# A decode step of two transformer layers: the last product of layer 1 is laid out by result columns, takes the residual in, and is written as four rows

## The chip, the cores and the metric

The program runs on one core of a Trainium2 chip. Its engines are TensorE (PE in the profile, with its weight loads listed as PEld), VectorE (DVE), ScalarE (ACT), GpSimd (POOL) and SyncE (SP); 16 DMA engines carry the core's transfers. The metric is the device time of one execution in microseconds, given as the median of several runs. Less is better.

## The reference

One token (a row x of 640 values, bfloat16) goes through two layers of attention and two of a gated feed-forward block. Both layers use the same weights and the same caches:

```
x = x + A(layernorm(x))      # layer 0
x = x + B(layernorm(x))
x = x + A(layernorm(x))      # layer 1
x = x + B(layernorm(x))
A: q = x @ wq (32 heads of 192); scores against the last 4096 keys of each head,
   softmax, weighted sum of the values, then @ wo
B: out = (silu(x @ w1) * (x @ w3)) @ w2       # w1, w3: 640 x 1536; w2: 1536 x 640
```

The change concerns the last line of the last layer: the product with w2, the sum with x, and the write of the 640 results.

## The kernel before

**Data.** All large operands stream from HBM through an arena of 16 slots in SBUF, each 128 partitions by 6144 bfloat16 values (1536 KB). A list `loads` fixes the order of the transfers; `refill` (L184 to L195) issues the next ones on SP's queue whenever a slot has come free, and `done` (L209) gives a slot back. For each layer the list holds the pages of wq, the K and V pages of 32 heads, six pages of wo, and four pages of the feed-forward weights: `fa` and `fb` (w1 and w3, first four fifths), `fc` (the rest of w1 and w3, and w2's chunks 0 to 3), and `fd` (w2's chunks 4 to 10). Chunk 11 of w2 stays in a buffer of its own, `keep`, from layer 0 on. A chunk is 128 rows of w2, 640 columns wide, 160 KB.

`fd` is loaded in two transfers, of 3840 columns (chunks 4 to 9, 960 KB) and of 640 columns (chunk 10, 160 KB). They are the last two loads of the program.

**The residual.** x is kept as `xsq[:, 0:5]` in float32: value 5p + c of x stands in partition p, column c.

**Products of one row.** With only one token, each product has a stationary operand of one column. TensorE's array is therefore used as four groups of 32 columns: `tile_position=(0, 32 * j)` places a product in group j, and its one row of results lands on PSUM partition 32j. In the w2 product (L421 to L431), chunk `fcx` goes to group `fcx % 4`; the 640 result columns are two halves of 320, each in a PSUM tile of its own. So every group holds a partial sum over three of the twelve chunks, for all 640 columns. `y_open` first fills the two tiles with a product of a zero operand, eight instructions of 320 columns, so that the other partitions are zero.

**From partial sums to the residual.** `y_to_residual` (L228 to L236) copies the two PSUM tiles to SBUF as bfloat16 (one on ScalarE, L230, one on VectorE, L231), multiplies the copy's columns with a column of ones in five small products (tile `yt_ps`), which adds the four partial rows and brings value 5p + c to partition p, column c, and adds `xsq` on VectorE (L235). In layer 1 this last sum goes to `ob`, bfloat16, 128 by 5, and one transfer on SP's queue (L474) writes it to HBM: 128 pieces of 10 bytes.

**Order.** `pin` keeps the instructions of each engine in the order of the program text, and each engine runs its own in that order, waiting on semaphores. All products are issued by the helper `mm`, so they all carry line L75; they are told apart by their tiles: `g_ps`, `u_ps` (products with w1 and w3), `gt_ps` (their transposes), `htd` (the gated values, bfloat16, 12 columns of 128, written by L418), `y_ps`, `yt_ps`, `st_ps` (the layer norm's sums, a float32 product), `rl_ps` (sums of the softmax, a float32 product). SP's queue issues loads alone until the output transfer. POOL writes constants at the start (L93 to L127) and later copies parts of `wst`; it has nothing to do in the last feed-forward block.

Of the kernel before, what the change touches and what calls it, by code (L numbers as in the profile page):

```python
# [7 lines left out]
BF16 = mybir.dt.bfloat16  # L8
F32 = mybir.dt.float32
U32 = mybir.dt.uint32  # L10
ALU = mybir.AluOpType
# [4 lines left out]
P = 128  # L16
D = 640
NCH = 5
# [6 lines left out]
PGW = 6144  # L25
# [17 lines left out]
def kernel(  # L43
# [13 lines left out]
    nc = tc.nc  # L57
# [3 lines left out]
    cst = ctx.enter_context(tc.tile_pool(name="cst", bufs=1))  # L61
# [3 lines left out]
    ps_a = ctx.enter_context(tc.tile_pool(name="ps_a", bufs=2, space=PSUM))  # L65
# [4 lines left out]
    def pin(ins):  # L70
        tc.keep_in_program_order(ins)
        return ins

    def mm(*a, **k):
        return pin(nc.tensor.matmul(*a, **k))  # L75
# [9 lines left out]
    xsq = cst.tile([P, 12], F32, name="xsq")  # L85
# [9 lines left out]
                            pattern=[[-32, 4]], channel_multiplier=1)  # L95
# [3 lines left out]
                            pattern=[[-32, 4], [-1, 4]], channel_multiplier=1)  # L99
# [4 lines left out]
    for j in range(4):  # L104
        nc.gpsimd.affine_select(out=sel[:], in_=sel[:], compare_op=ALU.not_equal, fill=1.0, base=-(32 * j + 14),
                                pattern=[[-1, 2], [2, HB], [0, 16]], channel_multiplier=1)
    lsel = cst.tile([64, HB, 16], F32, name="lsel")
    nc.gpsimd.memset(lsel[:], 0.0)
    for blk in range(8):
        nc.gpsimd.affine_select(out=lsel[:], in_=lsel[:], compare_op=ALU.not_equal, fill=1.0, base=-(8 * blk + 7),  # L110
                                pattern=[[1, HB], [0, 16]], channel_multiplier=1)
    mask = cst.tile([P, 16], BF16, name="mask")
    nc.gpsimd.memset(mask[:], 0.0)
    for hl in range(HB):
        nc.gpsimd.affine_select(out=mask[:], in_=mask[:], compare_op=ALU.not_equal, fill=1.0, base=-16 * hl,
                                pattern=[[-1, 16]], channel_multiplier=1)
# [6 lines left out]
    ptm = cst.tile([P, 16 * 144], BF16, name="ptm")  # L123
    otd = cst.tile([P, 48], BF16, name="otd")
    htd = cst.tile([P, 12], BF16, name="htd")
    zero = cst.tile([P, 32], BF16, name="zero")
    nc.gpsimd.memset(zero[:], 0.0)  # L127
    w20 = cst.tile([P, 768], BF16, name="w20")
    qt_sb = cst.tile([P, 2, 6, 16], BF16, name="qt_sb")


    cst.tile([P, 80], BF16, name="pad")
    arena = arn.tile([P, NSLOT * PGW], BF16, name="arena")
    keep = arn.tile([P, 640], BF16, name="keep")
    rest = arn.tile([P, PGW - NSTASH], BF16, name="rest")
    free = list(range(NSLOT))
    home = {}
    loads = []
# [5 lines left out]
    w2_v = B_w2.rearrange("(p f) n -> p (f n)", f=12)  # L144
# [12 lines left out]
    for layer in range(2):  # L157
        for c in range(NCH):
            loads.append((("q", layer, c), [(0, PGW, wq_v[c])]))
        for i in range(H + LEAD):  # L160
            for kind, g, cache in (("v", i - LEAD, A_v_cache), ("k", i, A_k_cache)):
                if not 0 <= g < H:
                    continue
                h = (k_head if kind == "k" else head)(layer, g)
                if kind == "k" and layer == 1 and h in RETAIN:
                    if h == STASH:
                        loads.append((("k", 1, h), []))
                    continue
                loads.append(((kind, layer, h),
                              [(0, PGW, cache[0, h, S0:SK, :].rearrange("(p t) d -> p (t d)", p=P))]))  # L170
        for w in range(6):
            parts, ci, end = [], 9 * w, min(9 * w + 9, 48)
            while ci < end:
                to = min(end, ci - ci % 12 + 12)
                parts.append((640 * (ci - 9 * w), 640 * (to - ci),
                              wo_v[ORDER[layer][ci // 12]][:, 640 * (ci % 12):640 * (ci % 12 + to - ci)]))
                ci = to
            loads.append((("o", layer, w), parts))
        loads.append((("fa", layer), [(0, PGW, w1_v[:, 0:PGW])]))
        loads.append((("fb", layer), [(0, PGW, w3_v[:, 0:PGW])]))  # L180
        loads.append((("fc", layer), [(0, 1536, w1_v[:, PGW:]), (1536, 1536, w3_v[:, PGW:]),
                                      (3072, 2560, w2_v[:, 0:2560])]))
        loads.append((("fd", layer), [(0, 3840, w2_v[:, 2560:6400]), (3840, 640, w2_v[:, 6400:7040])]
                      + [(None, 640, w2_v[:, 7040:7680])] * (layer == 0)))  # L184

    def refill():
# [18 lines left out]
    def page(key):  # L205
        return arena[:, home[key] * PGW:home[key] * PGW + PGW]

    def done(key):
        free.append(home.pop(key))  # L209
        refill()  # L210
# [14 lines left out]
        pin(nc.vector.tensor_scalar(out=xs[:, :, 3], in0=xsq[:, 0:NCH],  # L225
                                    scalar1=st[:, 0:1], scalar2=rstd[:], op0=ALU.subtract, op1=ALU.mult))

    def y_to_residual(y_ps, dst=None):  # L228
        y_sb = w20
        pin(nc.scalar.copy(out=y_sb[:, 0:320], in_=y_ps[0][:, 0:320]))  # L230
        pin(nc.vector.tensor_copy(out=y_sb[:, 320:640], in_=y_ps[1][:, 0:320]))  # L231
        yt_ps = ps_m.tile([P, NCH], F32, tag="m", name="yt_ps")
        for c in range(NCH):
            mm(yt_ps[:, c:c + 1], lhsT=y_sb[:, c:D:NCH], rhs=onesb[:], start=True, stop=True)
        pin(nc.vector.tensor_tensor(out=(xsq[:, 0:NCH] if dst is None else dst), in0=xsq[:, 0:NCH], in1=yt_ps[:],  # L235
                                    op=ALU.add))  # L236

    def qproj(layer):
        q_ps = ps_a.tile([P, 512], F32, tag="a", name="q_ps")
# [125 lines left out]
    def y_open(name):  # L365

        y_ps = [ps_a.tile([P, 512], F32, tag="a", name=f"{name}{i}") for i in range(2)]
        for nh in range(2):
            for j in range(4):
                mm(y_ps[nh][32 * j:32 * j + 32, 0:320], lhsT=zero[:], rhs=ptm[:, 0:320],  # L370
                   start=True, stop=False, tile_position=(0, 32 * j))
        return y_ps
# [12 lines left out]
            done(("o", layer, w))  # L385
        y_to_residual(y_ps)

    def ffn(layer, dst=None):
        g_ps = ps_a.tile([P, 512], F32, tag="a", name="g_ps")
        u_ps = ps_a.tile([P, 512], F32, tag="a", name="u_ps")  # L390
        for ps, kind, c0, c1, off in ((g_ps, "fa", 0, 4, 0), (u_ps, "fb", 0, 4, 0),
                                      (g_ps, "fc", 4, 5, 0), (u_ps, "fc", 4, 5, 1536)):
            pg = page((kind, layer))
            for c in range(c0, c1):
                for j in range(4):
                    mm(ps[32 * j:32 * j + 32, 0:384], lhsT=xs[:, c, 3:35],
                       rhs=_ap(pg, 0, P, off + 1536 * (c - c0) + 3 * j, [[12, 128], [1, 3]]),
                       start=(c == 0), stop=(c == NCH - 1), tile_position=(0, 32 * j))
            if kind != "fc":
                done((kind, layer))  # L400
        gu = w20.rearrange("p (g n) -> p g n", g=2)
        pin(nc.scalar.copy(out=gu[:, 0, :], in_=g_ps[:, 0:384]))
        pin(nc.vector.tensor_copy(out=gu[:, 1, :], in_=u_ps[:, 0:384]))
        gt_ps = ps_m.tile([P, 2, 3, 4], F32, tag="m", name="gt_ps")
        for gi in range(2):
            for k in range(3):
                mm(gt_ps[:, gi, k, :], lhsT=gu[:, gi, k:384:3], rhs=sel4[:], start=True, stop=True)
        ex = sml.tile([P, 12], F32, tag="ex", name="ex")
        pin(nc.scalar.activation(out=ex[:], in_=gt_ps[:, 0, :, :].rearrange("p k j -> p (k j)"), func=ACTF.Exp,
                                 scale=-1.0))  # L410
        ut = sml.tile([P, 12], F32, tag="ut", name="ut")
        pin(nc.vector.tensor_copy(out=ut[:], in_=gt_ps[:, 1, :, :].rearrange("p k j -> p (k j)")))
        gut = sml.tile([P, 12], F32, tag="gut", name="gut")
        pin(nc.vector.tensor_tensor(out=gut[:], in0=gt_ps[:, 0, :, :].rearrange("p k j -> p (k j)"), in1=ut[:],
                                    op=ALU.mult))
        pin(nc.vector.tensor_scalar_add(out=ex[:], in0=ex[:], scalar1=1.0))
        pin(nc.vector.reciprocal(out=ex[:], in_=ex[:]))
        pin(nc.vector.tensor_tensor(out=_ap(htd[:], 0, P, 0, [[1, 3], [3, 4]]),  # L418
                                    in0=gut[:].rearrange("p (k j) -> p k j", k=3),
                                    in1=ex[:].rearrange("p (k j) -> p k j", k=3), op=ALU.mult))  # L420
        y_ps = y_open("y2_ps")  # L421
        for fcx in range(12):
            j = fcx % 4
            pg, off = (page(("fc", layer)), 3072 + 640 * fcx) if fcx < 4 else (page(("fd", layer)), 640 * (fcx - 4))
            if fcx == 11:
                pg, off = keep, 0
            for nh in range(2):
                mm(y_ps[nh][32 * j:32 * j + 1, 0:320], lhsT=htd[:, fcx:fcx + 1], rhs=pg[:, off + 320 * nh:off + 320 * nh + 320],
                   start=False, stop=(fcx >= 8), tile_position=(0, 32 * j))
            if fcx == 3:  # L430
                done(("fc", layer))  # L431
        done(("fd", layer))
        y_to_residual(y_ps, dst)

    def attention(layer):
        layernorm()
# [29 lines left out]
        wo_proj(layer)  # L466

    refill()
    ob = cst.tile([P, NCH], BF16, name="ob")
    for layer in range(2):  # L470
        attention(layer)
        layernorm()
        ffn(layer, dst=(ob[:] if layer == 1 else None))
    nc.sync.dma_start(out=out[0, 0, :].rearrange("(p c) -> p c", c=NCH), in_=ob[:])  # L474


# [28 lines left out]
```

## Time and profile before

The kernel takes 537.86 us (median of three runs, 534.64 to 539.17). The profiled execution took 536.54 us; its span, from the first instruction to the last, is 534.4 us, so 2.1 us lie outside the span.

| | of the profiled execution |
|---|---|
| span | 534.4 us |
| DMA, mean over the span | 417 GB/s, 222.77 MB |
| PE busy | 288.6 us (54%) |
| DVE busy | 225.7 us (42%) |
| ACT busy | 41.8 us (8%) |
| POOL busy | 14.6 us (3%) |
| mean granted TensorE clock | 0.685 of full speed |

The DMA engines are busy for 90% or more in every fortieth of the span but the first (80%) and the last (30%). In the last 13 us the profile shows, from 521 us on, the gated products, the w2 product, the residual sum, and the output transfer, which is issued at 530.82 us. In the profile's rows, "x 8" is a count of instructions, "[0.71 <-DMA ...]" the idle time of the engine before the group and what ended it; the time of one matmul overlaps that of the next ones.

### The profile page before, as it was taken

Reading aid. Unit: us, or ns where it says so; the run is one execution under the profiler, and the core shown is the slowest. Engines: PE = TensorE matmul, PEld = TensorE weight load, DVE = VectorE, ACT = ScalarE, POOL = GpSimd, SP = SyncE. Lnnn points to the kernel's source line nnn. Section 1 sums busy time; section 2 is a strip of 40 time slices with the busy share of each in tenths; the row PEclk is TensorE's granted clock in tenths of the full one; section 3 lists DMA queues with packets and bytes.
Section 4 is the critical chain, followed back from the end, with each engine's and each line's share of the span. In section 5 each row is a group of like instructions: output and inputs, shape, how many; then the busy total and the mean of one; then the engine's idle time right before and its main releaser. Section 6 shows DMA issues by size and latency. Waiting matters only on the chain.

```text
span 534.4 us, 5680 instructions
## 1 busy us (share of the span) xinstructions
PE 288.6 (54%) x2400; PEld 118.7 (22%) x2400; DVE 225.7 (42%) x271; ACT 41.8 (8%) x107; POOL 14.6 (3%) x52
## 2 busy tenths in 40 slices
PE   2365364556554656553545366595556756734544
PEld 1121121222221222211212122252222222211121
DVE  1189765465455764520011058507444654410011
ACT  1100200011001100020000010203001100020000
POOL 5000000000000000000000000000000000000000
PEclk9989798657766575665556558887885776565556
DMA  8999999999999999999999999999999999999993
GB/s 347 429 430 429 432 426 430 428 431 431 426 432 426 433 427 430 430 418 432 421 415 418 428 373 407 425 428 431 432 426 429 428 433 428 428 429 430 428 421 153
DMA packets 22633, 222.77 MB, mean 417 GB/s; under 512 B 2768, under 2 KB 3152, under 8 KB 5456
## 3 DMA queue, kind: packets, MB, share of 16 engines
q1 hardware_dynamic: 22464, 222.41, 98.4%
q8 instruction: 19, 0.31, 0.2%
q14 instruction: 6, 0.05, 0.0%
q10 hardware_dynamic: 144, 0.00, 0.0%
HBM read 222.40 MB, written 0.00 MB: 416 GB/s over the span
## 4 chain that ended last, share of the span: by engine, by line
DMA 80%; PE 11%; DVE 6%; ACT 1%; issue 1%; POOL 0%; SPq 0%; DVEq 0%; ACTq 0%; POOLq 0%
DMA arena<-in_A_k_cache_dram 50%; DMA arena<-in_A_v_cache_dram 13%; DMA arena<-in_A_wo_dram 8%; DMA arena<-in_B_w_dram 5%; DVE arena L286 4%; PE s_ps L75 4%; DMA arena<-in_A_wq_dram 4%; PE pss L75 2%; PE o_ps L75 2%; DMA xb<-in_A_x_dram 1%; PE y_ps L75 1%; PE q_ps L75 1%; ACT w L316 0%; DVE t L301 0%; PE u_ps L75 0%
## 5 line engine op out<-in xcount | busy, mean ns | idle before, releaser
L286 DVE STREAM_TRANSPOSE arena<-arena 128x1536 uint32<-128x1536 uint32 x100 | 171.3, 1754 | 96.6 <-DMA arena<-in_A_k_cache_dram 96.4
L75 PE MATMUL pss<-arena,wst 128*32 128x512 bf16 x480 | 108.3, 539 | 107.4 <-DVE arena L286 104.7
L75 PE MATMUL o_ps<-arena,ptm 128*16 128x384 bf16 (+1 forms) x1024 | 124.8, 458 | 29.3 <-DMA arena<-in_A_v_cache_dram 27.6
L75 PEld LDWEIGHTS <-wst 128*32 128x32 bf16 x768 | 55.1, 116 | 234.7 <-issue 195.9
L75 PE MATMUL s_ps<-arena,wst 128*32 128x512 bf16 x288 | 54.7, 502 | 34.0 <-DVE arena L286 28.5
L75 PEld LDWEIGHTS <-ptm 128*16 128x16 bf16 (+2 forms) x1036 | 47.1, 107 | 72.9 <-issue 64.0
L359 DVE SCALAR_TENSOR_TENSOR w<-ot_ps,rl,mask 128x192 bf16<-128x192 f32 x8 | 3.3, 418 | 57.4 <-PE ot_ps L75 57.4
L75 PE MATMUL y_ps<-arena,otd 128*1 128x320 bf16 x192 | 17.2, 458 | 16.3 <-DMA arena<-in_A_wo_dram 16.3
L311 ACT ACTIVATE tb<-m 32x32 f32<-32x32 f32 x8 | 1.8, 228 | 297.7 <-DVE m L308 297.7
L75 PE MATMUL q_ps<-arena,xs 128*32 128x384 bf16 x160 | 14.5, 519 | 18.8 <-DMA arena<-in_A_wq_dram 16.1
L329 ACT COPY ptm<-w 32x128 bf16<-32x128 bf16 x40 | 16.1, 403 | 26.3 <-PE o_ps L75 24.1
L231 DVE CAST w<-y_ps 128x320 bf16<-128x320 f32 x4 | 2.0, 491 | 38.2 <-PE y_ps L75 38.2
L75 PEld LDWEIGHTS <-xs 128*32 128x32 bf16 x240 | 9.3, 125 | 36.9 <-issue 27.9
L256 DVE CAST ptm<-q_ps 128x768 bf16<-128x768 f32 x2 | 1.9, 958 | 31.7 <-ACT w L254 31.7
L275 POOL COPY wst<-qt_sb 32x48 bf16<-32x48 bf16 x16 | 6.2, 385 | 232.8 <-PE pss L75 188.0
L75 PEld LDWEIGHTS <-otd 128*1 128x1 bf16 x192 | 6.6, 102 | 26.8 <-issue 22.6
L301 DVE TENSOR_REDUCE t<-s_ps 64x1 f32<-64x512 f32 x3 | 2.0, 682 | 17.8 <-PE s_ps L75 17.8
L301 DVE TENSOR_REDUCE t<-pss 64x1 f32<-64x512 f32 x5 | 3.4, 681 | 12.9 <-PE pss L75 12.9
L319 DVE STREAM_TRANSPOSE w<-w 64x512 bf16<-64x512 bf16 x8 | 5.6, 705 | 7.2 <-ACT w L316 7.2
L75 PE MATMUL ot_ps<-w,sel 128*128 128x192 bf16 x16 | 3.4, 309 | 8.7 <-ACT w L353 7.9
L353 ACT CAST w<-o_ps 128x384 bf16<-128x384 f32 x8 | 3.8, 478 | 54.5 <-PE o_ps L75 51.7
L75 PE MATMUL st_ps<-xsq,onesD 128*128 128x12 f32 x8 | 2.3, 367 | 9.4 <-DVE xsq L213 9.4
(78 smaller groups left out, 101.2 us busy)
## 6 DMA issues: line engine op xcount, KB each, us to landing
arena<-in_A_v_cache_dram SPq DMA_DIRECT2D x64, 1536.0 KB, 29.2
arena<-in_A_k_cache_dram SPq DMA_DIRECT2D x50, 1536.0 KB, 29.2
arena<-in_A_wq_dram SPq DMA_DIRECT2D x10, 1536.0 KB, 10.5
arena<-in_A_wo_dram SPq DMA_DIRECT2D x6, 1440.0 KB, 15.9
arena<-in_B_w_dram SPq DMA_DIRECT2D x4, 1536.0 KB, 13.9
arena<-in_A_wo_dram SPq DMA_DIRECT2D x4, 960.0 KB, 16.6
arena<-in_A_wo_dram SPq DMA_DIRECT2D x6, 480.0 KB, 14.4
arena<-in_B_w_dram SPq DMA_DIRECT2D x2, 960.0 KB, 13.1
```

The lines of the kernel that those rows point to most:

```text
L75: return pin(nc.tensor.matmul(*a, **k))
L231: pin(nc.vector.tensor_copy(out=y_sb[:, 320:640], in_=y_ps[1][:, 0:320]))
L256: pin(nc.vector.tensor_copy(out=q_rep[par][:], in_=src))
L275: pin(nc.gpsimd.tensor_copy(out=dst, in_=src))
L286: pin(nc.vector.transpose(x[:, w * sp:w * (sp + 1)].bitcast(U32), x[:, w * sp:w * (sp + 1)].bitcast(U32)))
L301: pin(nc.vector.reduce_max(out=t0[:, 0:1], in_=s_ps[0:64, :], axis=AX.X))
L311: pin(nc.scalar.mul(out=tb[32:64, :].rearrange("p (a z) -> p a z", a=4), in_=mb, mul=-SCALE))
L319: pin(nc.vector.transpose(et[:], e[:]))
L329: pin((eng.copy if eng is nc.scalar else eng.tensor_copy)(out=dst, in_=src))
L353: pin(nc.scalar.copy(out=o_sb[:, 0:384], in_=o_ps[:, 0:384]))
L359: pin(nc.vector.scalar_tensor_tensor(out=om, in0=ot_ps[:], scalar=rl[:], in1=mask[:].unsqueeze(2).broadcast_to([P, 16, 12]), op0=ALU.mult, ...
```

## The change

Layer 0 is left as it is. In layer 1:

- The third load of `fd` appears: its 3840 columns come as 2560 (chunks 4 to 7) and 1280 (chunks 8 and 9), and then the 640 columns of chunk 10.
- A function `last_rows` takes the place of the w2 product, the two copies, the five `yt_ps` products, the sum on VectorE and the output transfer. Group j now takes result columns 160j to 160j + 159 of every chunk: twelve chunks by four groups, 48 products of 160 columns, all into one PSUM tile `f_ps`. Four products with a zero operand open it.
- x is added inside that tile: for each of the five columns c of `xsq` and each group j, a float32 product of `xsq[:, c]` with 32 columns of an identity matrix writes the values 5p + c of the group to every fifth column. These are 20 float32 products, each of 32 columns. They stand on PE after the `gt_ps` products and the zero products, and before the first product with `htd`.
- The identity, 128 by 128 float32, is made by two instructions on POOL, in the arena slot that has been free for longest; all loads have been issued by then.
- The chunks are taken in the order 0, 1, 2, 3, 11, 4, ..., 10.
- One copy on VectorE brings 128 partitions by 160 columns to SBUF as bfloat16, and one transfer on SP's queue writes partitions 0, 32, 64 and 96 to HBM: four rows of 320 bytes.
- The buffer `ob` is gone, and the unused buffer `pad` grows from 80 to 96 columns; the arena begins at the same address as before.

```
-        loads.append((("fd", layer), [(0, 3840, w2_v[:, 2560:6400]), (3840, 640, w2_v[:, 6400:7040])]
+        fd = [(0, 3840), (3840, 640)] if layer == 0 else [(0, 2560), (2560, 1280), (3840, 640)]
+        loads.append((("fd", layer), [(o, n, w2_v[:, 2560 + o:2560 + o + n]) for o, n in fd]
                       + [(None, 640, w2_v[:, 7040:7680])] * (layer == 0)))
...
+    def ffn(layer):
+        if layer == 1:
+            assert not loads
+            spare = free[0] * PGW
+            ident = arena[:, spare:spare + 256].bitcast(F32)
+            nc.gpsimd.memset(ident, 0.0)
+            nc.gpsimd.affine_select(out=ident, in_=ident, compare_op=ALU.not_equal, fill=1.0, base=0,
+                                    pattern=[[-1, P]], channel_multiplier=1)
...
+        if layer == 1:
+            return last_rows(ident)
...
+    def last_rows(ident):
+        f_ps = ps_a.tile([P, 512], F32, tag="a", name="f_ps")
+        for j in range(4):
+            mm(f_ps[32 * j:32 * j + 32, 0:160], lhsT=zero[:], rhs=ptm[:, 0:160], start=True, stop=False,
+               tile_position=(0, 32 * j))
+        for c in range(NCH):
+            for j in range(4):
+                mm(f_ps[32 * j:32 * j + 1, c:160:NCH], lhsT=xsq[:, c:c + 1], rhs=ident[:, 32 * j:32 * j + 32],
+                   start=False, stop=False, tile_position=(0, 32 * j))
+        for fcx in (0, 1, 2, 3, 11, 4, 5, 6, 7, 8, 9, 10):
+            pg, off = w2_chunk(1, fcx)
+            for j in range(4):
+                mm(f_ps[32 * j:32 * j + 1, 0:160], lhsT=htd[:, fcx:fcx + 1],
+                   rhs=pg[:, off + 160 * j:off + 160 * j + 160],
+                   start=False, stop=(fcx == 10), tile_position=(0, 32 * j))
+        row = w20[:, 0:160]
+        pin(nc.vector.tensor_copy(out=row, in_=f_ps[:, 0:160]))
+        ps = row.ap[0][0]
+        nc.sync.dma_start(out=out[0, 0, :].rearrange("(j i) -> j i", j=4),
+                          in_=bass.AP(row.tensor, row.offset, [[32 * ps, 4], [1, 160]]))
```

`w2_chunk` returns the page and the column where a chunk begins, as the lines of `ffn` did.

More of the change, by code (lines that the diff above doesn't have):

```diff
@@ L129 @@
     qt_sb = cst.tile([P, 2, 6, 16], BF16, name="qt_sb")
-    cst.tile([P, 80], BF16, name="pad")
+    cst.tile([P, 96], BF16, name="pad")
     arena = arn.tile([P, NSLOT * PGW], BF16, name="arena")
@@ L226, in layernorm, with y_to_residual @@
                                     scalar1=st[:, 0:1], scalar2=rstd[:], op0=ALU.subtract, op1=ALU.mult))
-    def y_to_residual(y_ps, dst=None):
+    def y_to_residual(y_ps):
         y_sb = w20
@@ L234, in y_to_residual @@
             mm(yt_ps[:, c:c + 1], lhsT=y_sb[:, c:D:NCH], rhs=onesb[:], start=True, stop=True)
-        pin(nc.vector.tensor_tensor(out=(xsq[:, 0:NCH] if dst is None else dst), in0=xsq[:, 0:NCH], in1=yt_ps[:],
-                                    op=ALU.add))
+        pin(nc.vector.tensor_tensor(out=xsq[:, 0:NCH], in0=xsq[:, 0:NCH], in1=yt_ps[:], op=ALU.add))
     def qproj(layer):
@@ L386, in wo_proj, with w2_chunk @@
         y_to_residual(y_ps)
-    def ffn(layer, dst=None):
+    def w2_chunk(layer, fcx):
+        if fcx == 11:
+            return keep, 0
+        return (page(("fc", layer)), 3072 + 640 * fcx) if fcx < 4 else (page(("fd", layer)), 640 * (fcx - 4))
+    def ffn(layer):
[6 more added lines that the diff above has]
+                                    pattern=[[-1, P]], channel_multiplier=1)
         g_ps = ps_a.tile([P, 512], F32, tag="a", name="g_ps")
@@ L423, in ffn @@
             j = fcx % 4
-            pg, off = (page(("fc", layer)), 3072 + 640 * fcx) if fcx < 4 else (page(("fd", layer)), 640 * (fcx - 4))
-            if fcx == 11:
-                pg, off = keep, 0
+            pg, off = w2_chunk(layer, fcx)
             for nh in range(2):
@@ L432, in ffn @@
         done(("fd", layer))
-        y_to_residual(y_ps, dst)
+        y_to_residual(y_ps)
+    def last_rows(ident):
[18 more added lines that the diff above has]
+                          in_=bass.AP(row.tensor, row.offset, [[32 * ps, 4], [1, 160]]))
     def attention(layer):
@@ L468 @@
     refill()
-    ob = cst.tile([P, NCH], BF16, name="ob")
     for layer in range(2):
@@ L472 @@
         layernorm()
-        ffn(layer, dst=(ob[:] if layer == 1 else None))
-    nc.sync.dma_start(out=out[0, 0, :].rearrange("(p c) -> p c", c=NCH), in_=ob[:])
+        ffn(layer)
 _INS = ['A_x', 'A_k_cache', 'A_v_cache', 'A_wq', 'A_wo', 'B_x', 'B_w1', 'B_w3', 'B_w2']
```

## The prediction

> **What bounds the kernel now.** I read the page's fortieths first. The DMA engines are busy nearly throughout, at 417 GB/s in the mean, and the 222 MB that they move stay the same. So the change can act only in what follows the loads. The chain of waits, read from its end, tells how long that is:
>
> ```profile
> 488.40 22.48 DMA arena<-in_A_wo_dram
> 510.91 0.03 issue
> 510.94 17.46 DMA arena<-in_B_w_dram
> 528.39 0.04 issue
> 528.44 1.16 PE y_ps L75 x16
> 529.62 0.50 DVE w L231
> 530.12 0.14 issue
> 530.25 0.35 PE yt_ps L75 x5
> 530.62 0.16 DVE ob L235
> ```
>
> The columns are start, duration, work. Until 528.39 us the chain consists of transfers; the one that ends there is the 960 KB transfer of w2's chunks 4 to 9. After it come 1.16 us of products and 1.2 us from the first copy to the output transfer. This transfer is in the view of the DMA issues, with the last load above it (KB each, us from issue to landing):
>
> ```profile
> arena<-in_B_w_dram SPq DMA_DIRECT2D x1, 160.0 KB, 14.4
> out_dram<-ob SPq DMA_DIRECT2D x1, 1.2 KB, 2.6
> ```
>
> The timeline places the 160 KB issue (chunk 10) at 514.35 us and the output's at 530.82 us. Chunk 10 therefore lands at 528.75, the results at 533.4, and 1.0 us is left to the span's end at 534.4. No more than some 6 us of the span are in reach of this change.
>
> For the price of small products I read the timeline of PE (start, duration of the group, count):
>
> ```profile
> 468.32 0.38 PE L75 MATMUL rl_ps<-l,lsel 64*128 64x1 f32 x2 [0.61 <-ACT w L316]
> ...
> 517.84 0.57 PE L75 MATMUL st_ps<-xsq,onesD 128*128 128x12 f32 x2 [0.55 <-DVE xsq L213]
> ...
> 525.96 0.46 PE L75 MATMUL y_ps<-ptm,zero 128*32 128x320 bf16 x8
> ...
> 527.28 0.45 PE L75 MATMUL y_ps<-arena,htd 128*1 128x320 bf16 x8 [0.86 <-DVE htd L418]
> ...
> 530.25 0.33 PE L75 MATMUL yt_ps<-onesb,w 128*128 128x1 bf16 x5 [0.71 <-DVE w L231]
> ```
>
> The step from one product to the next is the group's duration less that of one product, over the count less one. One `htd` product lasts 0.30 us at least, so its steps are (0.45 - 0.30)/7 = 21 ns at the clock of this moment. The 16 on the chain ran at (1.16 - 0.45)/15 = 47 ns. One `yt_ps` product lasts 0.178, so (0.33 - 0.178)/4 = 38 ns. Float32 is dearer: 0.57 - 0.37 = 0.20 us from the first to the second record for `st_ps`, 0.38 - 0.27 = 0.11 for `rl_ps`. The clock explains the 21 and the 47:
>
> ```profile
> 515.00:520.00 5.00, 2.36 (x31) 1.28 (x23) 1.50 (x6) 0.83 (x3) 0.00 (x0) 0.50 0.99 419
> ...
> 525.00:528.50 3.50, 1.51 (x30) 0.69 (x30) 1.39 (x6) 0.42 (x2) 0.00 (x0) 0.94 0.26 104
> 528.50:534.40 5.90, 1.38 (x21) 0.59 (x20) 0.65 (x2) 0.42 (x1) 0.00 (x0) 0.53 0.02 3
> ```
>
> Of the last three numbers of each row, the first is the granted clock: 0.94 up to 528.5 us, 0.53 after it.
>
> **What comes off the end.** Before, 530.82 - 529.62 = 1.20 us pass from the start of the copies to the output's issue: a copy of 320 columns (0.49 us on DVE), five products, the sum, and hand-overs. After, one copy of 160 columns stays. The copies of 384 columns (0.56) and 320 (0.49) differ by 1.1 ns a column, so it costs 0.49 - 160 x 0.0011 = 0.32 us; with 0.02 and 0.04 for the hand-overs, 0.38. Gain 0.82 us.
>
> **The output transfer.** It keeps its issue (0.35 us) and its landing, but has four pieces in place of 128. Between 531 and 532 us the trace has 140 packets of under 512 bytes, and most pass within 0.2 us, the last 0.35 us after the first. Gain between 0 and 0.35; I take 0.2, the dense part. A loss isn't excluded: the other 1.2 KB transfer, the load of x at the start, took 6.6 us to land, 4.0 more than this one, with a full queue beside it. The Trainium skill (DMA: Bandwidth & Descriptors, the section on why a DMA increments its semaphore by 16) says that the number of engines is the largest divisor, up to 16, of the slowest dimension, which makes it four here, with one row each; no trace of before shows such a transfer.
>
> **The products, up to the last one.** What was 8 + 24 products of 320 columns becomes 4 + 48 of 160: the same columns per group, twice the instructions. The step for 160 columns lies between 21 ns (seen with 320 columns at the fast clock) and 47 (at the slow one, which half the columns should nearly halve); I take 30. The 20 float32 products are the unknown. The layer norm runs four times and its product leaves 8 records, so each new one counts as two: 40 records. Their nearest rows differ both ways: `st_ps` (0.20) and `rl_ps` (0.11) are float32, but load 128 columns of weights against one here; `yt_ps` (0.038) has short moving data, but bfloat16; 21 ns is the bottom, as nothing on this page goes faster. I take 40 ns, the row nearest in length, since loading a single column is what the dear rows don't have. That makes 1.6 us, bounds 0.84 and 8.0.
>
> The Trainium skill (FP8 and Floating Point Precision, TensorE Precision Notes) speaks against this change here: true float32 takes four passes through the array. The profile records two per product; by the rule, with each pass at the price of a record, the phase would take 3.2 us and the whole sum would come out at +0.4 us instead of -1.2.
>
> Now in order. PE comes to the zero products at 525.96 as before; four take 0.12, up to 526.08. Float32 products up to 527.68. `htd` is ready at 527.22 (L418 starts at 527.03 and takes 0.19), so 0.46 us of the phase are no longer covered by that wait, while 1.14 lie in what was idle. Then 20 products (chunks 0 to 3, 11), 0.6 us: 528.28. Chunks 4 to 7 are the first two thirds of the transfer that landed at 528.39; the last 160 KB took 0.36 us, so the 320 KB split off take about 0.7, and they land at 527.7, before PE asks. 16 products: 528.76. Chunks 8 and 9 (528.39) are there: 529.0. Chunk 10 (528.75) too: 529.12, and the last product's own 0.30 makes it 529.42, against 529.60. Gain 0.2 us. What hides the float32 phase is the wait for `htd` and for data; without it, each 10 ns on a record cost 0.4 us.
>
> **Edits at nothing.** The identity: POOL had 0.33 us for its select and 0.20 for a memset on 64 x 128 float32, and no work after its copies into `wst`; the slot that has been free for longest held the sixth last V page, read by PE from 473.7 to 475.2 us, so the identity stands 50 us before it is read. Were POOL late, its 0.6 us would be added in full. SP issues one load more (0.33 us); it idles 15.3 us before the output, so nothing waits behind it. The last load moves one place back in the ring of completions that each issue waits for: its issue waits for the last wo transfer (480 KB, about 1.1 us at 430 GB/s) rather than for the one before, so about 515.5 instead of 514.35. Its landing took 14.4 us, nearly all of it queueing, which covers that; without the cover, 1.1 us. The wait of the identity products for POOL and the order of the chunks hold up only what is counted above. Layer 0 and the arena's addresses are unchanged.
>
> **Sum.** -0.82 - 0.2 - 0.2 = -1.2 us: the profiled execution's 536.54 would become 535.3. It lies 1.3 us below the median of the three runs; from that median, 537.86, I forecast 536.7.
>
> **Rivals.** (1) *The float32 products become the bound of the tail; slower.* They stand ahead of every `htd` product, and each record above 40 ns delays the end. The 1.2 us are used up at 2.8 us for the phase, 70 ns a record; from there on it is slower. At `rl_ps`' price the phase takes 4.4 us: 536.7 + 2.8 = 539.5. At `st_ps`' price, 8.0: 536.7 + 6.4 = 543.1. For it: both float32 rows of the trace lie above 70 ns. Against it: both load 128 columns, and the four groups can work side by side here. (2) *Data alone sets the end.* At 21 ns a record the phase takes 0.84 us; PE then waits for chunk 10 (528.75 + 0.05), does four products and ends at 529.2; with 0.35 us from the transfer the sum is -0.4 - 0.82 - 0.35 = -1.6: 536.3. (3) *The output transfer is dearer with four rows* than with 128 pieces: at the bound of 4.0 us, the gain of 0.2 gone, 540.9. (4) *The tail's gain isn't seen*, as the three runs of before lie 4.5 us apart and the median of the next ones falls anywhere in there.
>
> **Chances and range.** My forecast, data and float32 products about even, 0.50; rival 2 0.18; rival 1 0.22 (0.06 of it at `st_ps`' price); rival 3 0.04; something else, 0.06. Only the run spread reaches more than 1% (5.4 us, about what a measurement of this kernel can tell from no change) below: faster 0.08. Above it stand `st_ps`' price and the spread: slower 0.10; within, 0.82. For the range, the lowest run less 1.2 is 533.4, and rival 1 at `rl_ps`' price with some spread 540.2; I leave a little out below: 533.6 to 540.2.
>
> **What would show it.** Right: `f_ps` products of `xsq` from about 526.1 to 527.7; one DVE copy of 160 columns in 0.32 us; the output issued near 530 us and landing in 2.4 us. Wrong: float32 records above 70 ns, a gap on PE that a 2560- or 1280-column load ends after 528.4, a landing above 3 us, or any group ahead of 520 us that differs.

## The result and the profile after

The changed kernel takes 533.75 us (median of 22 runs, 531.26 to 536.28), the kernel before 535.51 us in as many runs (533.53 to 539.17). The ratio is 0.9954, 95% interval 0.9937 to 0.9971: a gain of 2.5 us, between 1.6 and 3.4 (the two medians lie 1.8 us apart). The direction was right, the gain by the ratio was twice the 1.2 us that I had forecast. That the time itself came out 3 us below the 536.7 has a second cause: the three runs shown ahead had a median of 537.86, 2.35 above that of all 22.

The profiled execution took 532.73 us, its span is 530.6. The end of its chain of waits (start, duration, work) answers to the nine lines of before:

```profile
513.89 13.39 DMA arena<-in_B_w_dram
527.28 0.04 issue
527.32 0.27 PE f_ps L75 x4
527.62 0.32 DVE w L463
```

The chain ends with the last load, chunk 10 (it landed 13.39 us after its issue, at 527.28), four products and one copy. Before, it left the loads one transfer earlier, at 528.39, as 16 products were still to be done. The timeline of the same execution shows what became of the products (start, duration of the group, count, and what ended the idle time before it):

```profile
524.51 0.51 PE L75 MATMUL f_ps<-arena,xsq 128*1 128x32 f32 x40
...
525.74 0.45 PE L75 MATMUL f_ps<-arena,htd 128*1 128x160 bf16 x16 [0.72 <-DVE htd L430]
...
526.91 0.66 PE L75 MATMUL f_ps<-arena,htd 128*1 128x160 bf16 x12 [0.35 <-DMA arena<-in_B_w_dram]
...
527.62 0.32 DVE L463 CAST w<-f_ps 128x160 bf16<-128x160 f32 x1 [1.93 <-PE f_ps L75]
...
528.00 0.65 SPq L465 DMA_DIRECT2D out_dram<-w  x1
```

The float32 products leave 40 records in 0.51 us, PE then waits 0.72 us for `htd`, and 0.35 us for the 1280 columns. So it is the data that PE waits for, not the other way round. The copy takes the 0.32 us that were worked out. The last wait of SP's queue, for the landing of the results, is in the view of the waits; first the kernel before, then the changed one (us in total, times, longest):

```profile
SPq L500 <- DMA out_dram<-ob: 2.2, 1, 2.2
```

```profile
SPq L531 <- DMA out_dram<-w: 0.9, 1, 0.9
```

Since the landing of the last load (issue plus time to landing) differs by 1.5 us between the two executions, I compare what follows it, in three pieces. Each kernel was profiled a second time:

| us | last landing to copy (DVE) | copy to the output's issue | issue to the span's end | sum |
|---|---|---|---|---|
| before | 0.87 | 1.20 | 3.58 | 5.65 |
| before, again | 0.81 | 1.20 | 4.33 | 6.34 |
| changed | 0.34 | 0.38 | 2.60 | 3.32 |
| changed, again | 0.33 | 0.39 | 2.61 | 3.33 |

The sum, called the tail from here on, is 2.33 us shorter in the first pair, which agrees with the 2.5 us of the ratio: 0.53 at the products, 0.82 between copy and issue, 0.98 behind the issue. In the second pair it is 3.01 us shorter, as the output transfer of before took longer there (more on this under the repetitions). The landings themselves (528.75 and 526.06 before, 527.28 and 528.97 after) lie up to 2.9 us apart without order; the runs spread by some microseconds too.

### The profile page after: what moved, and what is told of

The parts are those of the page before. It is cut to its first block, busy times and chain, and to the rows that moved or that the text cites. A ratio compares the mean times of both kernels' runs of the same rounds, so it can differ in the third digit from the quotient of the medians.

```text
span 530.6 us, 5792 instructions
## 1 busy us (share of the span) xinstructions
PE 290.4 (55%) x2455; PEld 119.8 (23%) x2455; DVE 225.4 (42%) x270; ACT 41.4 (8%) x106; POOL 15.1 (3%) x54
## 4 chain that ended last, share of the span: by engine, by line
DMA 79%; PE 10%; DVE 8%; ACT 1%; issue 1%; POOL 0%; SPq 0%; ACTq 0%; DVEq 0%; POOLq 0%
DMA arena<-in_A_k_cache_dram 45%; DMA arena<-in_A_v_cache_dram 18%; DMA arena<-in_A_wo_dram 7%; DVE arena L286 5%; PE s_ps L75 4%; DMA arena<-in_B_w_dram 4%; DMA arena<-in_A_wq_dram 3%; PE o_ps L75 2%; PE pss L75 1%; DMA xb<-in_A_x_dram 1%; PE y_ps L75 1%; DVE pss L202 1%; PE q_ps L75 1%; DVE t L301 1%; ACT w L316 0%
## 5 line engine op out<-in xcount | busy, mean ns | idle before, releaser
L75 PE MATMUL pss<-arena,wst 128*32 128x512 bf16 x480 | 110.6, 544 | 105.3 <-DVE arena L286 102.6
L75 PE MATMUL o_ps<-arena,ptm 128*16 128x384 bf16 (+1 forms) x1024 | 126.6, 460 | 28.9 <-DMA arena<-in_A_v_cache_dram 27.1
L75 PE MATMUL s_ps<-arena,wst 128*32 128x512 bf16 x288 | 53.4, 492 | 33.6 <-DVE arena L286 28.0
```

## The experiments

### The output transfer

The first two runs undo this part of the change alone (`out128`, upper half of the diff), and make it alone (`before_rows4`, lower half).

```
-        nc.sync.dma_start(out=out[0, 0, :].rearrange("(j i) -> j i", j=4),
-                          in_=bass.AP(row.tensor, row.offset, [[32 * ps, 4], [1, 160]]))
+        nc.sync.dma_start(out=out[0, 0, :].rearrange("(p c) -> p c", c=NCH),
+                          in_=bass.AP(row.tensor, row.offset, [[ps, P], [1, NCH]]))
...
-    nc.sync.dma_start(out=out[0, 0, :].rearrange("(p c) -> p c", c=NCH), in_=ob[:])
+    row = w20[:, 0:160]
+    nc.sync.dma_start(out=out[0, 0, :].rearrange("(j i) -> j i", j=4),
+                      in_=bass.AP(row.tensor, row.offset, [[32 * ps, 4], [1, 160]]))
```

> The changed kernel, but its output transfer has the old form: 128 partitions of 10 bytes, read from the first five columns of the same copy (so the sums of the other columns are not written). Measure: from the output's issue to the span's end, 3.6 us before and 2.6 us after the change. Theory A (the form of the transfer is worth 1.0 us, because many small writes are confirmed late): 3.6 us again, tail from the landing of chunk 10 to the span's end 4.3 us, whole time 1.0 us above the changed kernel. Rival B (the landing was quicker because it began when the queues had been quiet for longer, or by chance): 2.6 us, tail 3.3 us.

> The kernel before, with the new form of the output transfer alone: four rows of 320 bytes, read from the buffer of the partial sums, whose first five columns hold the results (so the other columns written are not the results). Theory A: from the output's issue to the span's end 2.6 us in place of 3.6, tail from the landing of chunk 10 to the end 4.65 us in place of 5.65; the whole time 1.0 us (0.2%) below before. Rival B: 3.6 and 5.65 us, same time.

Timeline and waits of the first (128 pieces of 10 bytes):

```profile
528.19 0.35 SPq L465 DMA_DIRECT2D out_dram<-w  x1
```

```profile
SPq L531 <- DMA out_dram<-w: 2.1, 1, 2.1
```

and of the second (four rows):

```profile
528.93 0.65 SPq L475 DMA_DIRECT2D out_dram<-w  x1
```

```profile
SPq L502 <- DMA out_dram<-w: 0.9, 1, 0.9
```

From the issue to the span's end the old form takes 531.7 - 528.19 = 3.51 us in the changed kernel, and the new one 531.6 - 528.93 = 2.67 us in the kernel before. So the form makes the difference, 0.8 to 1.0 us, in either surrounding: theory A. (The second tail, 4.88 us, is longer than the 4.65 expected: its copies began 0.95 us after the last landing rather than 0.87, and the two pieces behind them took 1.26 and 2.67.) The ratios to the kernel before are 0.9973 (0.9949 to 0.9997) and 0.9968 (0.9941 to 0.9995); each part alone is faster than before, and each interval holds what was expected (0.9973 and 0.9981). Two more forms tell which property it is: 16 rows of 80 bytes (`out16`), and 128 pieces of 10 bytes from four rows (`out128on4`).

```
+        nc.sync.dma_start(out=out[0, 0, :].rearrange("(p c) -> p c", c=40),
+                          in_=bass.AP(row.tensor, row.offset, [[8 * ps, 16], [1, 40]]))
...
+        nc.sync.dma_start(out=out[0, 0, :].rearrange("(a j c) -> j a c", j=4, c=NCH),
+                          in_=bass.AP(row.tensor, row.offset, [[32 * ps, 4], [NCH, 32], [1, NCH]]))
```

> The changed kernel with an output of 16 rows of 80 bytes from 16 partitions (15 of them don't hold the results of their place), so that all 16 DMA engines take part with one piece each. If the number and size of the pieces decide (A1), the landing stays quick: issue to end at most 2.7 us, perhaps 2.3, as the issue itself is 0.35 us again rather than 0.65. If the number of engines that have to report decides (A2), it is 3.4 to 3.6 us.

> The changed kernel with the four rows cut into 128 pieces of 10 bytes that are written in another order (so the 640 results stand permuted), on four DMA engines. A1 (number and size of the pieces): issue to end at least 3.6 us, more if 32 pieces on one engine take longer than 8. A2 (number of engines): 2.6 to 2.9 us.

The waits for the landing, of 16 rows and of 128 pieces on four engines:

```profile
SPq L531 <- DMA out_dram<-w: 1.0, 1, 1.0
```

```profile
SPq L531 <- DMA out_dram<-w: 2.5, 1, 2.5
```

Issue to end: 2.72 us for 16 rows, 4.24 for 128 pieces on four engines. The pieces decide (A1), not the number of engines: 10 bytes are slow on 16 engines and on four, 80 bytes are quick on 16 and 320 on four. The numbers of engines fit the packets that the trace counts after the issue, 144 in `out128`, 132 in `out128on4`, 32 in `out16` and 8 in the changed kernel: 128, 128, 16 and 4 pieces, and one packet more for each of 16, 4, 16 and 4 engines. Whether it is their size or their number these forms can't separate, as both go together. What I had expected of the issue itself was wrong: it took 0.59 us with 16 rows, not 0.35; only the form with 128 partitions is issued in 0.35.

### The float32 products

The edits, in this order: no identity products and nothing on POOL (`noident`), all in group 0 (`onegroup`), three times (`ident3`), six times (`ident6`).

```
-        for c in range(NCH):
+        for c in range(0):
...
-                mm(f_ps[32 * j:32 * j + 1, c:160:NCH], lhsT=xsq[:, c:c + 1], rhs=ident[:, 32 * j:32 * j + 32],
-                   start=False, stop=False, tile_position=(0, 32 * j))
+                mm(f_ps[0:1, c:160:NCH], lhsT=xsq[:, c:c + 1], rhs=ident[:, 32 * j:32 * j + 32],
+                   start=False, stop=False, tile_position=(0, 0))
...
+        for c in list(range(NCH)) * 3:
...
+        for c in list(range(NCH)) * 6:
```

> The changed kernel without the 20 identity products and without POOL's two instructions (x is not added). Measure: from the landing of chunk 10 to the span's end, 3.3 us in the changed kernel, and from the end of the gt products to the first htd product. Theory (the float32 products lie wholly in the wait for htd, 40 records in 0.51 us): nothing moves, tail 3.3 us. Rival (they delay the htd products or the last copy): tail 3.0 us or less.

> The changed kernel with all 20 identity products in column group 0 (so the results of the other groups lack x, and group 0 gets four groups' sums). If the four groups side by side make the record cheap, the step goes to about four times 8 ns, 32 ns, and the phase to 1.4 us. If the single column of weights does, it stays at 8 to 12 ns, 0.5 to 0.7 us. Either way the tail is 3.3 to 3.6 us.

Without them the tail is 3.4 us, 0.1 longer than with them: they cost nothing. With all of them in one column group, the timeline has

```profile
524.15 1.33 PE L75 MATMUL f_ps<-arena,xsq 128*1 128x32 f32 x40
```

(1.33 - 0.19)/39 = 29 ns a record in place of (0.51 - 0.19)/39 = 8 ns (one record lasts 0.19). Both phases had the full clock; in `out128`, at 0.68, the 40 records took 0.66 us, some 12 ns each. The four groups side by side make them cheap, as expected, and the phase is hidden even so: tail 3.38 us.

> The changed kernel with the identity products made six times (x is added six times): 240 records. Theory (8 ns a record, as read from the profile): 0.19 + 239 x 0.008 = 2.1 us from their start, so the htd products begin 0.9 us later than they could; at about 15 ns a product they are through by the time chunk 10 lands or up to 0.4 us later: tail 3.3 to 3.7 us. Rival (the records only look short, and what is queued behind them pays, at the 40 ns I had taken): 9.6 us for 240 records, tail 11 us.

> The changed kernel with the identity products made three times (x is added three times): 120 records. If a record costs 8 to 9 ns and the two gaps of six times were a matter of the supply of instructions: 0.19 + 119 x 0.0085 = 1.2 us without a gap, inside the wait for htd, tail 3.3 to 3.4 us. Rival (any longer run of such products stalls): a gap of PE of 1 us or more, tail 4 us or more.

Six times was meant to show the price where it is no longer hidden, and showed something else: a tail of 8.7 us, which neither side had forecast. Its timeline:

```profile
525.60 1.43 PE L75 MATMUL f_ps<-arena,xsq 128*1 128x32 f32 x150
...
529.67 1.38 PE L75 MATMUL f_ps<-arena,xsq 128*1 128x32 f32 x89 [2.65 <-issue]
...
533.67 0.37 PE L75 MATMUL f_ps<-arena,htd 128*1 128x160 bf16 x10 [1.32 <-issue]
```

and that of three times, with a tail of 4.4 us:

```profile
525.68 1.18 PE L75 MATMUL f_ps<-arena,xsq 128*1 128x32 f32 x120
...
527.28 0.37 PE L75 MATMUL f_ps<-arena,htd 128*1 128x160 bf16 x10
...
529.32 0.51 PE L75 MATMUL f_ps<-arena,htd 128*1 128x160 bf16 x18 [1.67 <-issue]
```

The price holds: 120 records in 1.18 us, expected 1.2. The rest of the expectation fell: by its gap and its tail the rival came true, though the gap isn't among the float32 products. PE stops for 2.65, 1.32 and 1.67 us with nothing to wait for ("issue"), in the middle of the float32 products in one kernel and of the `htd` products in the other. Counting two instructions for a weight load and its product, with two such pairs for each float32 product, the place is the same: 8 for the zero products + 300 for 150 records, and 8 + 240 + 60 for 30 products; 308 in both. The next stop comes 180 + 76 = 256 instructions later. So I supposed that instructions arrive in pieces of 256 and that PE had outrun them. The last kernel moves that place into the unchanged tail of the changed kernel, by 144 instructions in layer 0:

```
+        for k in range(72):
+            mm(y_ps[0][32 * (k % 4):32 * (k % 4) + 32, 0:8], lhsT=zero[:], rhs=ptm[:, 0:8], start=False, stop=False,
+               tile_position=(0, 32 * (k % 4)))
```

> The changed kernel with 72 additional zero products of 8 columns in layer 0 (144 instructions of PE, no effect on the result), the last feed-forward block of layer 1 unchanged. In the runs with the identity products three and six times PE stopped at the same place of its program, 308 instructions after the start of the zero products, and again 256 after that. If instructions come in pieces of 256 and PE outruns the next piece (supply): the place is now 164 after the start, so the last 10 products with htd stand behind a gap of 1.3 to 2.7 us that the profile puts down to issue; tail 4.6 us or more in place of 3.3. If the gaps came from the many float32 products themselves: no gap, tail 3.3 us.

There is no gap, and the tail is 3.3 us: as I had put it, the supposition fell. Pieces of 256 may still be right, if the next piece needs some 4 us and is asked for when PE enters the one before: between the entry into a piece (computed from the count) and the end of the gap lie 3.5 to 4.0 us in the three cases. In this last kernel the same count has PE enter the piece before at the start of the `g_ps` products (517.22 us), more than 9 us ahead of the place (526.7 us).

The DMA part of the page shows more. Beside the queue of the loads it lists one of kind "instruction"; for six times (packets, MB, share of 16 engines):

```profile
q8 instruction: 20, 0.33, 0.2%
```

That is 16 KB a packet; 20 packets of 256 instructions would be 5120, and PE ran 5310 products and weight loads in this execution. With six times such a packet passes at 527.41 us and another at 530.79, with three times one at 527.02; PE goes on 2.3, 2.9 and 2.3 us later. In the last kernel the packets pass at 518.65 and 527.08, so the first is 8 us ahead of the place. This kernel then didn't let PE outrun its instructions, and is no test of the supposition. That the gaps are a wait for instructions is likely by these times, not shown: the profile doesn't name the engine that a packet is for, and why PE needs over 2 us more after it stays open.

### The loads, the order and the clock

`oldloads` is the changed kernel with the two old loads and the old order of chunks; `before_split` is the kernel before with the new ones:

```
+        fd = [(0, 3840), (3840, 640)]
...
+        for fcx in range(12):
...
+        fd = [(0, 3840), (3840, 640)] if layer == 0 else [(0, 2560), (2560, 1280), (3840, 640)]
...
+        for fcx in (range(12) if layer == 0 else (0, 1, 2, 3, 11, 4, 5, 6, 7, 8, 9, 10)):
```

> The changed kernel with the loads and the order of chunks of before: 3840 columns in one transfer, chunk 11 last. Theory (the earlier part of the product hides behind the transfers because of the split): 28 products or more after the landing of the 960 KB piece, eight after chunk 10's, tail 0.1 to 0.4 us longer, 3.4 to 3.7 us. Rival (split and order don't matter): 3.3 us.

> The kernel before with the new loads and order of chunks alone (2560, 1280 and 640 columns; chunk 11 after chunk 3), still with columns of 320. Measure: from the landing of chunk 10 to the start of the copies, 0.87 us before, 0.34 after the change, and the clock granted meanwhile. Theory (what counts is how few products wait for the last landing: 2 of 320 columns or 4 of 160): 0.35 to 0.5 us at either clock. Rival (the column layout makes the products themselves quicker): 0.7 us or more.

In the first, the products after the last landing take 0.42 us in place of 0.34, and the tail is 3.48 us: 0.08 for the products and some spread (in the kernels with the new loads and an undisturbed tail the 0.34 lies between 0.31 and 0.38). In the second they take 0.72 us (0.87 before), although only two products were to wait for the last landing. By its number the rival had won; but the windows of the profile show why it was slow. For the last products of three kernels (columns: stretch, its length, busy time of PE, PEld, DVE, ACT, POOL with counts, then the granted clock): the kernel before,

```profile
528.44:529.62 1.18, 1.10 (x16) 0.38 (x15) 0.00 (x1) 0.00 (x0) 0.00 (x0) 0.65 0.00 0
```

the one with split loads,

```profile
526.36:527.69 1.33, 1.29 (x12) 0.30 (x6) 0.00 (x0) 0.21 (x1) 0.00 (x0) 0.50 0.01 4
```

and the changed one:

```profile
526.91:527.62 0.71, 0.55 (x12) 0.24 (x11) 0.00 (x1) 0.00 (x0) 0.00 (x0) 0.89 0.01 2
```

At 0.50 PE hadn't finished the chunks that had long landed: it ran from 525.32 without a wait and was the bound itself. Two kernels were to tell the clock from the order of the groups. In `before_turns` the groups take turns; `before_busy` makes the identity of the change and, after `y_open`, its 20 products:

```
+        for fcx, nh in [(4 * q + j, nh) for q in range(3) for nh in range(2) for j in range(4)]:
...
+            for c in range(NCH):
+                for j in range(4):
+                    mm(pss[32 * j:32 * j + 1, c:160:NCH], lhsT=xsq[:, c:c + 1], rhs=ident[:, 32 * j:32 * j + 32],
+                       start=True, stop=True, tile_position=(0, 32 * j))
```

> The kernel before with its 24 products of 320 columns in another order alone: the four groups take turns (chunks 0 to 3 for the left half, then for the right half, and so on) instead of two products in a row on each group. Measure: 16 products after the landing of the 960 KB piece, 1.16 us in the profile of before (1.11 in its repetition), the clock granted meanwhile, and landing of chunk 10 to the copies, 0.81 to 0.87 us. If turns make the products quick as in the changed layout (turns): about 0.75 us and 0.4 to 0.5 us, at whatever clock. If the clock does (clock): 0.75 us only where 1.0 is granted throughout, 1.1 us or more where it falls to 0.5.

> The kernel before with the 20 identity products of the change as mere occupation of PE, into a PSUM tile that nobody reads, after the zero products. In five profiles without them the fast clock lasted one stretch of 3.4 us in the tail and was over or nearly over when the last products ran; in nine with them it went on for longer in five. If the products keep the clock up (clock): 1.0 granted up to the copies, the 16 products in 0.75 to 0.9 us. If not, 0.5 by then and 1.1 us or more. By the theory of turns 1.1 us at either clock.

The windows of the 16 products, with turns and with the occupied PE:

```profile
527.30:528.18 0.88, 0.84 (x16) 0.28 (x15) 0.00 (x0) 0.08 (x1) 0.00 (x0) 1.00 0.00 0
```

```profile
526.40:527.30 0.90, 0.82 (x16) 0.38 (x15) 0.00 (x1) 0.00 (x0) 0.00 (x0) 1.00 0.00 0
```

Both got the full clock, and with it the 16 products take the same time with turns and without, 0.88 and 0.90 us; at 0.65 they take 1.18, at 0.72 (before, again) 1.14, at 0.50 (`before_rows4`) 1.34. So the order of the groups does nothing, and the clock does it. From the last landing to the copy the old layout needs 0.53 to 0.56 us at full clock; the 0.2 us that the new one is quicker even so are not the clock's.

That the identity products hold the clock up is likely, not shown: while the last products ran, the clock was 0.89 or more in all eleven profiles that have them, and in one of six without them (0.65, 0.72, 0.50, 0.50, 0.50, 1.00), `before_turns`. But the start of the fast stretch counts too: it lasted 3.41, 6.83 or 10.24 us, and in three of the eleven (the changed kernel, `out128`, `oldloads`) only 3.41, as in five of the six; there it reached the last products because it began late enough. The new layout hardly cares: without them, at 0.50, it needed 0.34 us as well.

### The repetitions

> The kernel before once more, for the spread of its tail: if the terms read from one trace are properties of the kernel, landing of chunk 10 to copies 0.8 to 1.0 us, start of the copies to the output's issue 1.2 us, issue to end 3.5 to 3.6 us, while everything up to the landing may lie 2 us off. If they are chance, they differ by 0.3 us or more.

> The changed kernel once more, for the spread of its tail: if the terms are properties of the kernel, landing of chunk 10 to copy 0.3 to 0.4 us, copy to the output's issue 0.38 us, issue to end 2.6 to 2.7 us. If they are chance, they differ by 0.3 us or more.

Their numbers are in the table above. Copy and products repeat within 0.06 us. The output transfer repeats in the changed kernel (2.60 and 2.61 us), not before: 3.58 and 4.33, where the wait for the landing was 2.9 us rather than 2.2:

```profile
SPq L500 <- DMA out_dram<-ob: 2.9, 1, 2.9
```

The packets say where the 0.7 us come from. In the second execution 135 of the 144 pass from 528.90 to 529.10 us, and the last nine, the share of one engine, from 530.16 to 530.24. An instruction packet of 16 KB had begun at 528.79 and taken 1.38 us, up to 530.17; very likely the nine stood behind it on their engine. So 4.33 is chance, not the form. The form of 10 bytes on 16 engines took 3.5 to 3.6 us in four other profiles, those of 80 or 320 bytes 2.6 to 2.7 in all.

## Why the prediction was right or wrong

The forecast was -1.2 us, the tail of the first pair lost 2.33. Of the 1.1 us between them, 0.78 are the output transfer's and 0.33 the products'.

**What bounds the kernel; right.** Only the tail could move, and what it lost accounts for the gain. No difference ahead of the last landing stands out of the spread.

**Copy to issue: -0.82 us; right.** 1.20 us became 0.38, in both pairs. The price of the copy, taken from the rows of 384 and 320 columns, was met: 0.32.

**The output transfer: -0.2 us; the larger of the two steps that failed.** The sign was right, the mechanism was not, and the size was 0.98 (0.8 to 1.0 in the two runs that change it alone). I had written that the transfer "keeps its issue (0.35 us) and its landing", and counted only the packets, which pass within 0.2 to 0.35 us. Neither was kept. The issue grew to 0.65 us, and the wait behind the packets shrank: before, the output's issue ends at 531.17 and the queue waits 2.2 us more, with the last packet at 532.02; after, the packets pass at 529.25 to 529.33 and the queue's wait is over at 528.65 + 0.9 = 529.55. Some 1.4 us between the last packet and the landing have become 0.2. Why short pieces wait so long stays open. The Trainium skill (DMA: Bandwidth & Descriptors, Anatomy of one DMA, a section on transfers issued by GpSimd) says that a fixed part of about 2.0 us is dominated by the receipt of the last write. A long wait after the last packet fits that; but for this transfer, issued by SP, it isn't fixed: from the end of the issue to the landing the same 1280 bytes took 0.9 us as rows and 2.1 as pieces of 10 bytes, and the measurement decides. My bound of a loss, 4.0 us from the load of x, had no counterpart.

**The products: -0.2 us; the step that failed is the price of a float32 record.** I took 40 ns from `yt_ps` and called 21 ns the bottom "as nothing on this page goes faster". It is 8 ns in four groups and 29 in one. `st_ps`, `rl_ps` and `yt_ps` load 128 columns of weights for every product, and the 21 ns came from products in four groups, but of 320 columns against 32; none could bound this case from below. So the phase took 0.51 us rather than 1.6, wholly inside the wait for `htd`, and the rest of my order of events (PE late at every landing, end 0.67 us after chunk 10's) fell with it. PE was early, and the end came 0.34 us after the landing. As to the products that was rival 2, to which I gave 0.18; its sum of -1.6 us had the output transfer too small as well. The four passes for true float32 that I weighed against the change left two records per product, and no trace of a longer phase.

What I left out is the clock: I had shown it at 0.53 for the last products of before, but used it only to choose a step. At full clock the old layout needs 0.53 to 0.56 us after the landing and the gain would have been 0.2; the other 0.3 of the 0.53 is what the lower clock cost the 16 products that stood behind the last landings. The new layout has four products left there, so that it has little to lose. The clock explains the size of the gain, not the miss: the sum took the old end, 529.60, from the trace, with the low clock in it.

**Edits at nothing; right.** The identity was made at 477.7 to 478.3 us by POOL, 46 us ahead of its use. The last load was issued 1 us closer to its landing than before (13.4 us ahead of it, not 14.4), as expected, and neither this nor the third load shows a cost beyond the spread. The split and the order are worth 0.08 us at the products, little more than the spread.

**The rivals.** The slower one, float32 products as the bound, didn't come true at any of its prices.

## What to carry to other kernels

Where results leave a kernel in its last microseconds, give the output transfer a few rows of 80 bytes or more rather than one short piece per partition: here that alone was worth 0.8 to 1.0 us, and what it saves isn't in the packets but in the wait behind them. Arrange the last product so that few instructions stand behind the last landing; whatever is left there also runs at whatever clock PE has been granted by then (the 16 products of before took 0.88 to 1.34 us). A price for small products holds only for their kind and their column groups: ask of each row whether its instructions could run side by side before calling it a bound.

## What the runs showed of the hardware that I had not expected

Float32 products with one column of weights, spread over the four column groups, follow each other at 8 ns a record at the full clock, 16 ns a product. The Trainium skill (TensorE: Matmul & The Clock Gate, in the section on 56 and 53.3 ns) says that the step between starts never falls below about 25 ns; the 29 ns in one group agree with it, the 8 ns in four do not.

The issue of a small transfer took 0.35 us with 128 partitions, and 0.59 to 0.70 us with 16 or four rows, in all profiles.

PE stopped for 1.3 to 2.7 us at places of its instruction stream that lie 256 instructions apart, when very short products had come in dense runs of over a hundred records. It went on 2.3 to 2.9 us after a 16 KB packet of an instruction queue; where the packet came 8 us early, PE didn't stop. The changed kernel ends 124 instructions short of the first of these places by the count above, so these runs don't tell whether it would stop there.

Instruction packets may also delay results: one of 16 KB that took 1.38 us stood ahead of the output transfer's packets in the second execution of before, and a sixteenth of them passed 1.1 us after the others. That they shared an engine is likely, not shown.
